# Attention with beacons and a soft mixture of experts: V loaded in fp16 through GpSimd's queue, its key order restored on TensorE, and TensorE's work in a new order

## The chip, the cores and the metric

The kernel runs on one core of one Trainium2 chip. The metric is device time in microseconds (us) of one execution. Before the change three runs gave 215.09, 217.38 and 217.65 us; the median is 217.38.

## The reference, cut to what matters

```
B, H, S, Nb, D = 8, 8, 576, 16, 64            # batches, heads, tokens, beacons, head width
k_all = concatenate([beacon_k, k], axis=2)    # 592 keys
v_all = concatenate([beacon_v, v], axis=2)
scores = q @ k_all.T / sqrt(D), causal over the 576, beacons always seen
a = softmax(scores);  attn = a @ v_all
x = attn as (B*S = 4608, H*D = 512)
logits = x @ phi                              # 32 slots, 4 for each of 8 experts
slot_input = softmax(logits over tokens).T @ x
slot_out = relu(slot_input[e] @ w1[e]) @ w2[e]   # w1 (512, 1024), w2 (1024, 512)
out = softmax(logits over slots) @ slot_out
```

All inputs and the output are float32.

## The kernel before

**Staging.** A batch has eight heads; they go in pairs, so there are 32 pairs, n = 0 to 31, and g = n % 4 is the pair's place in its batch. Keys are in five chunks of up to 128 (16 beacons and 576 tokens, the last chunk 80). `load_pair` (line 86) brings q and k of a pair on SyncE's queue; five pairs are in flight. `transp` (216) turns them on TensorE in bf16 into a PSUM buffer each, from which VectorE copies them to `qT` and `kT`, with the beacons' part from `bkT` (line 228). `bkT` is made once at the start by `beacons` (201), from `bkf`.

**Scores and attention.** `score(n, st)` (232) has four steps, which share two PSUM tiles `scs` in turn: step 2 needs what exp of step 0 has read, step 0 of the next pair what exp of step 2 has read. ScalarE takes exp of each step into `ex[n]`; GpSimd masks the diagonal blocks after steps 0 and 1. `attend(n, a)` (257) multiplies the 15 blocks of one head with `vh`, which holds V in fp16 and a column of ones per head; VectorE takes the reciprocal of the sums and scales into `xb`. Attention of pair n - 1 runs in iteration n.

**V.** `load_v` (100) loads V in float32 in the key order that attention needs, one chunk at a time: partition = key, so each packet is one row of 64 numbers, 256 bytes, on SyncE's queue. Beacon V comes apart. `cast_v` (277) turns each chunk to fp16 in `vh`: odd chunks on VectorE, even ones on GpSimd.

**Routing.** When a batch's eight heads are in `xb`, seven pieces follow (`routing`, 340): two transposes of two chunks (`xt_piece`) and one of the last, two halves of the logits with exp, the transposed weights (`dt_piece`) and the slot inputs (`si_piece`). They are queued in `work` and taken out between steps 0 and 1 of later iterations (lines 362 to 364): two in g = 1, three in g = 2, two in g = 3.

**PSUM.** Four banks hold the scores, two the attention, and two (`ps_tr`, tag `tr`, two buffers) are shared in turn by all transposes, logits and slot inputs.

**Weights.** `load_w` (129) loads the experts' weights with a cast to fp16 on GpSimd's queue, 24 full pieces during the loop after the schedule `want` (352), and 16 half pieces after the last iteration into buffers that q, k and V have left.

**The order** of every engine's work is the order of the program (`manual_schedule`, line 49); each engine takes its instructions in that order. The loop is in lines 357 to 404. After it come the experts (lines 408 to 460) and the output (464 to 478).

Of the kernel before, what the change touches and what calls it, by code (L numbers as in the profile page):

```python
# [17 lines left out]
def kernel(  # L18
# [12 lines left out]
    nc = tc.nc  # L31
# [37 lines left out]

    const = ctx.enter_context(tc.tile_pool(name="const", bufs=1))  # L70
    qkp = ctx.enter_context(tc.tile_pool(name="qkp", bufs=5))
    vfp = ctx.enter_context(tc.tile_pool(name="vfp", bufs=6))
    vbp = ctx.enter_context(tc.tile_pool(name="vbp", bufs=1))
    exq = ctx.enter_context(tc.tile_pool(name="exq", bufs=2))
    sml = ctx.enter_context(tc.tile_pool(name="sml", bufs=4))
    NW = 24
# [21 lines left out]
    vf = {}  # L98

    def load_v(b, cs):  # L100
        for c in cs:
            t = vfp.tile([P, H, D], FP, name="vf", tag="vf")
            vf[(b, c)] = t
            if c == 0 and b > 0:
                r0 = b * H * S - Nb
                nc.sync.dma_start(
                    out=t[:, :, :],
                    in_=v.rearrange("b h s d -> (b h s) d")[r0:r0 + H * S].rearrange(
                        "(h s) d -> s h d", s=S)[0:P])
            else:  # L110
                lo, hi = max(0, c * P - Nb), min(S, (c + 1) * P - Nb)
                p0 = lo + Nb - c * P
                nc.sync.dma_start(out=t[p0:p0 + hi - lo],
                                  in_=v[b, :, lo:hi, :].rearrange("h p d -> p h d"))
            if c == 0:
                vb = t
                if b > 0:
                    vb = vf[(b, "b")] = vbp.tile([P, H, D], FP, name="vb", tag="vb")
                nc.sync.dma_start(out=vb[0:Nb], in_=beacon_v[b].rearrange("h n d -> n h d"))

    NPC = 4 * E
    NH = 2 * (NPC - NW)
    wv = {}
    homes = ["qf", "kf", "vf", "vf"] * 2 + ["qf", "kf"] * 3 + ["vf", "vf"]
    assert len(homes) == NH

    def load_w(x):
        if x < NW:  # L130
            m, hs = x, (0, 1)
            t = wh.tile([P, 2048], F16, name="w", tag="w")
        else:
            m, hs = NW + (x - NW) // 2, ((x - NW) % 2,)
            tag = homes[x - NW]
            t = (vfp if tag == "vf" else qkp).tile(
                [P, 1024 if tag == "vf" else J * P], F16, name="wx", tag=tag)
# [18 lines left out]
    def w2c(e, t):  # L156
        o = (t % 2) * Dm
        return wv[(4 * e + 2 + t // 4, (t % 4) // 2)][:, o:o + Dm]

    load_pair(0)  # L160
    bkf = const.tile([P, B, D], FP, name="bkf")
    nc.sync.dma_start(out=bkf[:, :, :], in_=beacon_k.rearrange("b h n d -> (h n) b d"))
    load_pair(1)
    load_v(0, range(NCH))
# [4 lines left out]
    load_pair(4)  # L169


    idb = const.tile([P, P], BF, name="idb")
    make_identity(nc, idb)
# [103 lines left out]
    def cast_v(b, c):  # L277
        kn = P if c < 4 else UL
        (nc.vector if c % 2 else nc.gpsimd).tensor_copy(  # L279
            out=vh[b % 2][0:kn, c, :, 0:D], in_=vf.pop((b, c))[0:kn])  # L280
        if c == 0 and b > 0:
            nc.gpsimd.tensor_copy(out=vh[b % 2][0:Nb, 0, :, 0:D], in_=vf.pop((b, "b"))[0:Nb])
# [69 lines left out]
    def want(n):
        if n < 27:
            return int(0.66 * n)
        return {27: 19, 28: 21, 29: 23, 30: NW}.get(n, NW + NH)

    for n in range(NP + 1):
        b, g = divmod(n, H // 2)
        last = n == NP
        if not last:  # L360
            score(n, 0)
            for _ in range((0, 2, 3, 2)[n % 4]):
                if work:
                    work.pop(0)()
            score(n, 1)
# [9 lines left out]
        if not last:  # L375
            score(n, 2)
        if n >= 1:
            attend(n - 1, 1)
            if n % (H // 2) == 0:
                work += routing(n // (H // 2) - 1)  # L380
        if not last:
            score(n, 3)
        if last:
            while work:
                work.pop(0)()

        if not last:
            if g == 3 and b + 2 < B:
                load_v(b + 2, (0,))
            if b + 1 < B:  # L390
                load_v(b + 1, ((0, 1) if n == 0 else (1,), (2,), (3,), (4,))[g])
            if n + 5 < NP:
                load_pair(n + 5)
            if g == 0 and b > 0:
                cast_v(b, 3)
                cast_v(b, 4)
            if g == 2 and b + 1 < B:
                cast_v(b + 1, 0)
                cast_v(b + 1, 1)
            if g == 3 and b + 1 < B:  # L400
                cast_v(b + 1, 2)
            while wl < want(n):
                load_w(wl)
                wl += 1
    assert wl == NW + NH
# [103 lines left out]
```

## Time and profile before

| | |
|---|---|
| three runs | 215.09, 217.38, 217.65 us |
| the profiled execution | 215.74 us, of which the span on the engines is 214.0 |
| mean granted TensorE clock | 0.898 |
| DMA | 61,795 packets, 43,072 of them under 512 B; 55.86 MB |
| SyncE's queue (q, k, V, out) | 52,928 packets, 38.58 MB |
| GpSimd's queue (weights) | 8,832 packets, 16.78 MB |

Busy time by stage, us (each stage's length in brackets), with the granted clock of TensorE:

| stage | TensorE | VectorE | ScalarE | GpSimd | clock |
|---|---|---|---|---|---|
| 0 to 12 (12) | 4.15 | 5.80 | 2.44 | 2.86 | 1.00 |
| 12 to 20 (8) | 6.63 | 6.91 | 5.25 | 4.35 | 1.00 |
| 20 to 60 (40) | 34.75 | 29.12 | 30.36 | 20.38 | 0.96 |
| 60 to 100 (40) | 35.68 | 30.91 | 30.54 | 21.25 | 1.00 |
| 100 to 150 (50) | 43.90 | 38.48 | 36.08 | 28.50 | 0.97 |
| 160 to 185 (25) | 21.51 | 4.53 | 2.60 | 7.85 | 0.64 |
| 185 to 214 (29) | 12.51 | 13.41 | 11.72 | 0.00 | 0.68 |

How to read the lines of a profile: a group of instructions is given with its source line, its engine, the operation, what it writes and reads (partitions x elements), how often it occurs, the total and the mean time, and the idle time of the engine just before it with what ended that wait. In order of time a line begins with start and length in us. A matmul's end is modelled and neighbouring ones overlap, so the spacing of starts tells more of TensorE than the sum of lengths.

### The profile page before, as it was taken

Reading aid. Unit: us, or ns where it says so; the run is one execution under the profiler, and the core shown is the slowest. Engines: PE = TensorE matmul, PEld = TensorE weight load, DVE = VectorE, ACT = ScalarE, POOL = GpSimd, SP = SyncE. Lnnn points to the kernel's source line nnn. Section 1 sums busy time; section 2 is a strip of 40 time slices with the busy share of each in tenths; the row PEclk is TensorE's granted clock in tenths of the full one; section 3 lists DMA queues with packets and bytes.
Section 4 is the critical chain, followed back from the end, with each engine's and each line's share of the span. In section 5 each row is a group of like instructions: output and inputs, shape, how many; then the busy total and the mean of one; then the engine's idle time right before and its main releaser. Section 6 shows DMA issues by size and latency. Waiting matters only on the chain.

```text
span 214.0 us, 8069 instructions
## 1 busy us (share of the span) xinstructions
PE 168.1 (79%) x3512; PEld 118.0 (55%) x3512; DVE 135.5 (63%) x339; ACT 127.5 (60%) x187; POOL 90.0 (42%) x144
## 2 busy tenths in 40 slices
PE   0579985989989888998798799899986799898200
PEld 0447664666667666766566676676764745333000
DVE  4576996378678967877797786769655300189400
ACT  2076983679778777876767787766871011189300
POOL 5052924554465463375535644658545430000000
PEclk9999999699999999999999999969999655569855
DMA  6999999999999999999999999999999999169996
GB/s 188 246 280 256 302 264 270 279 272 240 296 311 237 261 292 300 249 291 243 261 293 280 290 257 278 308 202 196 194 211 182 209 209 206 24 281 404 406 408 266
DMA packets 61795, 55.86 MB, mean 261 GB/s; under 512 B 43072, under 2 KB 43072, under 8 KB 61760
## 3 DMA queue, kind: packets, MB, share of 16 engines
q1 hardware_dynamic: 52928, 38.58, 61.3%
q0 software_dynamic: 8832, 16.78, 43.0%
q8 instruction: 27, 0.44, 0.8%
q14 instruction: 8, 0.07, 0.1%
HBM read 62.69 MB, written 9.44 MB: 337 GB/s over the span
## 4 chain that ended last, share of the span: by engine, by line
PE 43%; DVE 26%; ACT 11%; DMA 6%; issue 5%; POOL 1%; DVEq 0%; SPq 0%; ACTq 0%
ACT ex L244 11%; PE sc L238 10%; PE tr L223 7%; PE av L265 6%; DVE xb L273 5%; DVE qT L225 4%; DVE xT L300 4%; DVE kT L225 4%; PE tr L310 4%; PE av L433 4%; DMA vf<-in_v_dram 4%; PE tr L425 4%; PE tr L295 3%; PE fp L471 2%; PE tr L333 2%
## 5 line engine op out<-in xcount | busy, mean ns | idle before, releaser
L244 ACT ACTIVATE ex<-sc 128x1024 f16<-128x1024 f32 (+3 forms) x128 | 106.8, 869 | 45.1 <-PE sc L238 44.7
L246 POOL TENSOR_SCALAR_AFFINE_SELECT ex<-ex 128x1024 f16<-128x1024 f16 x32 | 34.9, 1090 | 51.0 <-ACT ex L244 51.0
L238 PE MATMUL sc<-qT,kT 64*128 64x128 bf16 (+5 forms) x576 | 47.8, 260 | 10.7 <-ACT ex L244 5.1
L265 PE MATMUL av<-vh,ex 128*128 128x65 f16 (+2 forms) x960 | 45.4, 200 | 3.0 <-POOL vh L279 1.9
L265 PEld LDWEIGHTS <-ex 128*128 128x128 f16 (+2 forms) x960 | 37.5, 108 | 9.9 <-issue 8.1
L225 DVE COPY qT<-tr 128x576 bf16<-128x576 bf16 x32 | 24.2, 756 | 21.9 <-PE tr L223 21.7
L238 PEld LDWEIGHTS <-kT 64*128 64x128 bf16 (+1 forms) x576 | 20.9, 103 | 24.9 <-issue 16.1
L273 DVE TENSOR_TENSOR xb<-av,r 128x320 f16<-128x320 f32 x64 | 31.5, 492 | 2.2
L225 DVE COPY kT<-tr 128x576 bf16<-128x576 bf16 x32 | 23.9, 748 | 0.1
L279 POOL CAST vh<-vf 128x512 f16<-128x512 f32 (+1 forms) x24 | 14.6, 611 | 15.4 <-DMA vf<-in_v_dram 15.4
L146 POOL DMA_DIRECT2D w<-in_moe_w_dram x24 | 17.3, 720 | 0.0
L223 PE MATMUL tr<-idb,kf 64*64 64x64 bf16 x576 | 15.6, 198 | 1.4 <-DVE bkT L210 0.4
L223 PEld LDWEIGHTS <-qf 64*64 64x64 bf16 x576 | 12.6, 112 | 6.1 <-issue 4.5
L223 PE MATMUL tr<-idb,qf 64*64 64x64 bf16 x576 | 15.8, 199 | 0.1
L272 DVE RECIPROCAL r<-av 128x5 f32<-128x5 f32 x64 | 12.1, 189 | 5.8 <-PE av L265 5.6
L223 PEld LDWEIGHTS <-kf 64*64 64x64 bf16 x576 | 13.6, 113 | 2.5 <-issue 2.2
L473 ACT ACTIVATE osb<-fp,rc 128x512 f32<-128x512 f32 x18 | 11.7, 685 | 5.1 <-PE fp L471 4.4
L252 POOL TENSOR_SCALAR_AFFINE_SELECT ex<-ex 80x160 f16<-80x160 f16 x32 | 10.3, 323 | 10.1 <-ACT ex L244 7.9
L471 PE MATMUL fp<-soh,eLh 128*128 128x512 f16 x36 | 12.2, 452 | 2.2 <-ACT osb L473 1.3
L476 DVE TENSOR_SCALAR osb<-fp,rc 128x512 f32<-128x512 f32 x18 | 12.7, 747 | 1.8 <-PE fp L471 1.4
L295 PE MATMUL tr<-idh,xb 128*128 128x128 f16 (+1 forms) x160 | 12.3, 218 | 1.1 <-DVE xb L273 0.8
L146 POOL DMA_DIRECT2D wx<-in_moe_w_dram x16 | 8.5, 544 | 8.0 <-DMA wx<-in_moe_w_dram 5.2
(57 smaller groups left out, 139.5 us busy)
## 6 DMA issues: line engine op xcount, KB each, us to landing
w<-in_moe_w_dram POOLq DMA_DIRECT2D x24, 512.0 KB, 8.5
qf<-in_q_dram SPq DMA_DIRECT2D x32, 288.0 KB, 7.4
kf<-in_k_dram SPq DMA_DIRECT2D x32, 288.0 KB, 6.9
out_dram<-osb SPq DMA_DIRECT2D x18, 512.0 KB, 5.4
vf<-in_v_dram SPq DMA_DIRECT2D x31, 256.0 KB, 6.9
wx<-in_moe_w_dram POOLq DMA_DIRECT2D x16, 256.0 KB, 9.7
vf<-in_v_dram SPq DMA_DIRECT2D x8, 160.0 KB, 7.2
bkf<-in_beacon_k_dram SPq DMA_DIRECT2D x1, 256.0 KB, 3.9
```

The source lines that it names most:

```text
L146: nc.gpsimd.dma_start(out=t[:, 0:1024 * len(hs)].rearrange("p (c f) -> p c f", f=1024), in_=src)
L223: nc.tensor.transpose(tp[po:po + 64, j, :], hi, idb[po:po + 64, po:po + 64])
L225: nc.vector.tensor_copy(out=dst[:, Nb:Nb + S].rearrange("p (s j) -> p s j", j=J), in_=tp[:, :, :].rearrange("p j s -> p s j"))
L238: nc.tensor.matmul(sc[0:kn, a, col:col + un], kT[n % 3][64 * a:64 * a + 64, P * c:P * c + kn], qT[n % 3][64 * a:64 * a + 64, u0:u0 + un], ...
L244: nc.scalar.activation(ex[n][:, :, o:o + w], sc[:, :, 0:w], AF.Exp, scale=scale)
L246: nc.gpsimd.affine_select(out=ex[n][:, :, 0:512].rearrange("p a (c t) -> p a c t", c=4), in_=ex[n][:, :, 0:512].rearrange("p a (c t) -> p ...
L265: nc.tensor.matmul(avs[a][0:m, i * DD:(i + 1) * DD], ex[n][0:kn, a, o:o + m], vh[b % 2][0:kn, c, h, :], start=(c == 0), stop=(c == i))
L273: nc.vector.tensor_tensor(out=xb[b % 2][:, :, h, :], in0=avv[:, :, 0:D], in1=r5[:, :].unsqueeze(2).broadcast_to([P, NCH, D]), op=AL.mult)
L279: (nc.vector if c % 2 else nc.gpsimd).tensor_copy(out=vh[b % 2][0:kn, c, :, 0:D], in_=vf.pop((b, c))[0:kn])
L295: nc.tensor.transpose(tp[:, ii, t, 0:m], xb[b % 2][0:m, i, 2 * t:2 * t + 2, :].rearrange("p h d -> p (h d)"), idh[0:m, 0:m])
L471: nc.tensor.matmul(fp_[:, :], etok(cg, j), soh[:, :], start=True, stop=True)
L476: nc.vector.tensor_scalar(out=osb[:, j - j0, :], in0=fp_[:, :], scalar1=rc[:, i:i + 1], scalar2=None, op0=AL.mult)
```

## The change

V is loaded by `load_v` as a tile `vq` of 128 partitions with four neighbouring keys each, cast to fp16 on the way, by two DMAs per batch on GpSimd's queue; each packet reads 1 KB. It covers the first four chunks; the last 80 keys (`vl`) still come in float32 on SyncE's queue and GpSimd casts them. For batches after the first the tile starts 16 rows early, so that partition p holds keys 4p to 4p + 3 of the concatenated order; for the first batch it starts at partition 4 (124 partitions). Since key 4p + s lies in partition p, chunk c is in partitions 32c to 32c + 31, and `sel_piece` brings it in order: for each s a product with a 0/1 matrix `sel` (32 rows, 128 columns) over all 512 numbers of the eight heads, four products added up in PSUM, for two chunks at a time in alternation, and VectorE copies the sums to `vh`. Beacon V comes by eight DMAs on GpSimd's queue at the start and is copied into its 16 places by VectorE. `sel` is made at the start by a memset, four fills on GpSimd and a last memset of its first four rows on VectorE.

The loop is written anew. Step 0 of the next pair is issued at the end of an iteration, before the loads; attention stands behind steps 2 and 3 rather than ahead of them; the seven pieces of routing have places of their own (`slot`): ahead of step 1 ("pre"), ahead of step 3 ("mid") and at the end ("end"). `sel_piece` stands at the end of g = 2 and g = 3, for the next batch; for the first batch both stand in iteration 0 ahead of step 2. Two more weight pieces (26 in all) go into full-size buffers, 12 half pieces remain.

```diff
-    vfp = ctx.enter_context(tc.tile_pool(name="vfp", bufs=6))
-    vbp = ctx.enter_context(tc.tile_pool(name="vbp", bufs=1))
+    vqp = ctx.enter_context(tc.tile_pool(name="vqp", bufs=2))
+    vlp = ctx.enter_context(tc.tile_pool(name="vlp", bufs=2))
...
+    def load_v(b):
+        t = vqp.tile([P, H, 4, D], F16, name="vq", tag="vq")
+        vq[b] = t
+        p0 = Nb // 4 if b == 0 else 0
+        if b == 0:
+            nc.vector.memset(t[0:32], 0.0)
+        r0 = b * H * S - (Nb if b > 0 else 0)
+        rows = v.rearrange("b h s d -> (b h s) d")[r0:r0 + H * S].rearrange(
+            "(h p j) d -> p h j d", h=H, j=4)[0:P - p0]
+        for h0 in range(0, H, H // 2):
+            nc.gpsimd.dma_start(out=t[p0:P, h0:h0 + H // 2], in_=rows[:, h0:h0 + H // 2])
...
+    idb = const.tile([P, P], BF, name="idb")
+    make_identity(nc, idb)
     load_pair(0)
+    bvh = const.tile([P, 2, H, D], F16, name="bvh")
+    for b in range(B):
+        o = 32 * (b % 4)
+        nc.gpsimd.dma_start(out=bvh[o:o + Nb, b // 4], in_=beacon_v[b].rearrange("h n d -> n h d"))
+    load_v(0)
...
+    sel = const.tile([P, 4, P], F16, name="sel")
+    nc.vector.memset(sel[:, :, :], 0.0)
+    for c in range(4):
+        nc.gpsimd.affine_select(
+            out=sel[32 * c:32 * c + 32, :, :], in_=sel[32 * c:32 * c + 32, :, :],
+            compare_op=AL.not_equal, fill=1.0, base=0, pattern=[[-1, 4], [1, P]],
+            channel_multiplier=-4)
+    nc.vector.memset(sel[0:Nb // 4, :, :], 0.0)
...
+    def sel_piece(b, cs):
+        t = vq[b]
+        tps = [ps_tr.tile([P, H, D], FP, name="tr", tag="tr") for c in cs]
+        for s in range(4):
+            for c, tp in zip(cs, tps):
+                nc.tensor.matmul(tp[:, :, :], sel[32 * c:32 * c + 32, s, :],
+                                 t[32 * c:32 * c + 32, :, s, :],
+                                 start=(s == 0), stop=(s == 3))
+        for c, tp in zip(cs, tps):
+            nc.vector.tensor_copy(out=vh[b % 2][:, c, :, 0:D], in_=tp[:, :, :])
+        if 0 in cs:
+            o = 32 * (b % 4)
+            nc.vector.tensor_copy(out=vh[b % 2][0:Nb, 0, :, 0:D], in_=bvh[o:o + Nb, b // 4])
...
+    def place(b):
+        n0 = (b + 1) * (H // 2)
+        for i, (dn, w) in enumerate(((1, "mid"), (1, "end"), (2, "pre"), (2, "mid"), (3, "mid"),
+                                     (4, "pre"), (4, "mid"))):
+            places[(n0 + dn, w)] = routing(b)[i]
...
+    score(0, 0)
+    for n in range(NP):
         b, g = divmod(n, H // 2)
...
+        slot(n, "pre")
+        score(n, 1)
         if n + 1 < NP:
             transp(n + 1)
         if n == 0:
-            for c in range(NCH):
-                cast_v(0, c)
+            cast_vl(0)
+            sel_piece(0, (0, 1))
+            sel_piece(0, (2, 3))
...
+        score(n, 2)
         if n >= 1:
             attend(n - 1, 0)
-        if not last:
-            score(n, 2)
+        slot(n, "mid")
+        score(n, 3)
         if n >= 1:
             attend(n - 1, 1)
...
+            if g == 0:
+                place(b - 1)
+        slot(n, "end")
+        if g >= 2 and b + 1 < B:
+            sel_piece(b + 1, ((0, 1), (2, 3))[g - 2])
+        if n + 1 < NP:
+            score(n + 1, 0)
+
+        if n == 0:
+            load_v(1)
+        if g == 2 and b + 2 < B:
+            load_v(b + 2)
+        if g == 0 and b + 1 < B:
+            load_vl(b + 1)
...
```

More of the change, by code (lines that the diff above doesn't have):

```diff
@@ L94, in load_pair @@
             d[n] = t
[L98 to L119, printed above, removed]
+    vq, vl = {}, {}
@@ L123, with load_vl @@
+    def load_vl(b):
+        t = vlp.tile([P, H, D], FP, name="vl", tag="vl")
+        vl[b] = t
+        nc.sync.dma_start(out=t[0:UL], in_=v[b, :, S - UL:S, :].rearrange("h p d -> p h d"))
     NPC = 4 * E
-    NH = 2 * (NPC - NW)
+    NV = NW + 2
     wv = {}
-    homes = ["qf", "kf", "vf", "vf"] * 2 + ["qf", "kf"] * 3 + ["vf", "vf"]
-    assert len(homes) == NH
+    homes = ["qf", "kf"] * 5 + ["vl", "vl"]
+    NH = len(homes)
+    assert NH == 2 * (NPC - NV)
     def load_w(x):
-        if x < NW:
+        if x < NV:
@@ L131, in load_w @@
             m, hs = x, (0, 1)
-            t = wh.tile([P, 2048], F16, name="w", tag="w")
+            t = (wh if x < NW else vqp).tile([P, 2048], F16, name="w", tag="w" if x < NW else "vq")
         else:
[L134 to L137, printed above, removed]
+            m, hs = NV + (x - NV) // 2, ((x - NV) % 2,)
+            tag = homes[x - NV]
@@ L138, in load_w @@
+            t = (vlp if tag == "vl" else qkp).tile(
+                [P, 1024 if tag == "vl" else J * P], F16, name="wx", tag=tag)
         e, r = divmod(m, 4)
@@ L163 @@
     load_pair(1)
-    load_v(0, range(NCH))
+    load_vl(0)
     phif = const.tile([P, NDC, NSL], FP, name="phif")
@@ L169 @@
     load_pair(4)
-    idb = const.tile([P, P], BF, name="idb")
-    make_identity(nc, idb)
     idh = const.tile([P, P], F16, name="idh")
     nc.vector.tensor_copy(out=idh[:, :], in_=idb[:, :])
+    sel = const.tile([P, 4, P], F16, name="sel")
[6 more added lines that the diff above has]
+    nc.vector.memset(sel[0:Nb // 4, :, :], 0.0)
     ones = const.tile([P, 1], F16, name="ones")
@@ L275, in attend, with cast_vl @@
             in1=r5[:, :].unsqueeze(2).broadcast_to([P, NCH, D]), op=AL.mult)
[L277 to L282, printed above, removed]
+    def cast_vl(b):
+        nc.gpsimd.tensor_copy(out=vh[b % 2][0:UL, 4, :, 0:D], in_=vl.pop(b)[0:UL])
+    def sel_piece(b, cs):
[11 more added lines that the diff above has]
+            nc.vector.tensor_copy(out=vh[b % 2][0:Nb, 0, :, 0:D], in_=bvh[o:o + Nb, b // 4])
     xT = {}
@@ L344, in routing, with slot @@
                 lambda: dt_piece(b), lambda: si_piece(b)]
+    places = {}
+    def place(b):
[3 more added lines that the diff above has]
+            places[(n0 + dn, w)] = routing(b)[i]
+    def slot(n, w):
+        f = places.pop((n, w), None)
+        if f is not None:
+            f()
     beacons()
     transp(0)
-    work = []
     wl = 0
@@ L354, in want @@
             return int(0.66 * n)
-        return {27: 19, 28: 21, 29: 23, 30: NW}.get(n, NW + NH)
-    for n in range(NP + 1):
+        return {27: 19, 28: 21, 29: 23, 30: 25}.get(n, NV + NH)
+    score(0, 0)
+    for n in range(NP):
         b, g = divmod(n, H // 2)
-        last = n == NP
-        if not last:
[L361 to L365, printed above, removed]
+        slot(n, "pre")
+        score(n, 1)
         if n + 1 < NP:
@@ L368 @@
         if n == 0:
-            for c in range(NCH):
-                cast_v(0, c)
+            cast_vl(0)
+            sel_piece(0, (0, 1))
+            sel_piece(0, (2, 3))
             for r in range(4):
                 nc.vector.tensor_copy(out=phih[:, :, r, :], in_=phif[:, :, :])
+        score(n, 2)
         if n >= 1:
             attend(n - 1, 0)
-        if not last:
-            score(n, 2)
+        slot(n, "mid")
+        score(n, 3)
         if n >= 1:
             attend(n - 1, 1)
[L379 to L405, printed above, removed]
+            if g == 0:
[11 more added lines that the diff above has]
+            load_vl(b + 1)
+        if n + 5 < NP:
+            load_pair(n + 5)
+        if g == 3 and b + 1 < B:
+            cast_vl(b + 1)
+        while wl < want(n):
+            load_w(wl)
+            wl += 1
+    attend(NP - 1, 0)
+    slot(NP, "pre")
+    attend(NP - 1, 1)
+    slot(NP, "mid")
+    assert not places
+    for f in routing(B - 1):
+        f()
+    assert wl == NV + NH
     dsum = const.tile([P, 1], FP, name="dsum")
```

## The prediction

> **What bounds the kernel now.** I read the page's shares first, then the waits, then the instructions in order of time in the middle of the run and at its start.
>
> ```profile
> PE 168.1 (79%) x3512; PEld 118.0 (55%) x3512; DVE 135.5 (63%) x339; ACT 127.5 (60%) x187; POOL 90.0 (42%) x144
> DMA  6999999999999999999999999999999999169996
> ```
>
> No engine is full over the span, and the DMA engines are nearly always busy. Whether anybody waits for them is read from the waits (total us, times, longest):
>
> ```profile
> ACT ex L244 <- PE sc L238: 44.7, 69, 8.8
> POOL vh L279 <- DMA vf<-in_v_dram: 15.4, 6, 5.2
> PE av L265 <- POOL vh L279: 1.9, 1, 1.9
> ```
>
> GpSimd's wait for V reaches TensorE once, for 1.9 us. The 44.7 us in which ScalarE waits for scores are the loss. One iteration of the head-pair loop shows how they arise:
>
> ```profile
> 69.83 0.40 PE L238 MATMUL sc<-qT,kT 64*128 64x128 bf16 x8 [0.23 <-ACT ex L244]
> 70.17 1.19 PE L295 MATMUL tr<-idh,xb 128*128 128x128 f16 x16
> 70.35 1.02 ACT L244 ACTIVATE ex<-sc 128x1024 f16<-128x1024 f32 x1 [0.16 <-PE sc L238]
> 70.95 1.29 DVE L300 COPY xT<-tr 128x1024 f16<-128x1024 f16 x2 [0.21 <-PE tr L295]
> 71.28 0.41 PE L238 MATMUL sc<-qT,kT 64*80 64x80 bf16 x6
> 71.73 1.00 ACT L244 ACTIVATE ex<-sc 128x992 f16<-128x992 f32 x1 [0.36 <-PE sc L238]
> 72.29 0.47 PE L223 MATMUL tr<-idb,kf 64*64 64x64 bf16 x18
> 72.69 0.67 PE L265 MATMUL av<-vh,ex 128*128 128x65 f16 x15
> 73.30 0.37 PE L238 MATMUL sc<-qT,kT 64*128 64x464 bf16 x2
> 73.71 1.35 ACT L244 ACTIVATE ex<-sc 128x928 f16<-128x928 f32 x2 [0.97 <-PE sc L238]
> ```
>
> Routing (line 295) stands between step 0 and step 1 of the scores; its copies hold both `tr` buffers, so the transposes of k (72.29) wait; step 2 comes late and ScalarE idles 0.97. The step-0 products start at 66.39, 69.83, 74.70, 80.04 and (exp of step 2 ends there) about 84.75: the iteration without routing takes 3.44 us, those with it 4.87, 5.34 and 4.7, together 18.4 per group of four. So the loop is bound by TensorE's order and its hand-overs, not by DMA.
>
> **The change part by part.** V's DMA: 256-byte packets (most of the 43,072 under 512 B) become a quarter as many of 1 KB. By the waits above nobody but GpSimd stood behind them, save at 34 to 36 us, where ScalarE lost 3.05. I count this edit at nothing; its cover is the issue five iterations ahead of q and k and 7.4 us to land. If the cover failed it would be worth that 3 us. The casts of V leave VectorE (two of 478 ns per batch) and GpSimd (three of about 610 and one of 606; one stays).
>
> **The start.** Here the change adds a wait.
>
> ```profile
> 1.44 2.02 POOL L192 MEMSET hTz<- 128x2048 f16 x1
> 5.68 0.76 DVE L204 CAST bkd<-bkf 128x512 bf16<-128x512 f32 x2 [1.78 <-DMA bkf<-in_beacon_k_dram]
> 10.19 1.02 PE L238 MATMUL sc<-qT,kT 64*128 64x128 bf16 x14 [0.93 <-DVE kT L228]
> 12.25 0.91 PE L238 MATMUL sc<-qT,kT 64*128 64x464 bf16 x4
> 14.51 1.02 PE L238 MATMUL sc<-qT,kT 64*128 64x128 bf16 x14 [1.35 <-DVE kT L228]
> ```
>
> GpSimd now issues eight DMAs of beacon V and two of V before it fills `sel`. Its rows: 544 ns for a DMA of 128 packets, 720 for one of 256, so 1.4 ns per packet more. Eight of 128 packets: 4.3 us; two of 496: 544 + 368 x 1.4 = 1.06 each, 2.1. One fill of `sel` (512 elements, between 323 ns for 160 and 1,090 for 1,024): 0.64. From 1.4 us on, that ends at 8.4. VectorE's clearing of `sel[0:4]` waits for it, and behind it in VectorE's queue stand the memsets (some 0.75 us) and the casts of `bkf`: 9.2 instead of 5.68. From there to the first scores is a chain (casts, transposes, copies), so they shift by **+3.5** (0 if the wait is passed over, +5.4 if all four fills are waited for).
>
> In iteration 0 TensorE must now do both `sel_piece` calls before step 2, in its order. No row shows a 32-row product with 512 columns. Nearest are line 433's products (512 columns, four side by side): eight take 1.04 us, one 0.62, so a round takes 0.42 at the granted clock of 0.50 there, and 0.21 at full clock. The 464-column pair on 64 rows each (two in 0.37, one in 0.385) shows row halves side by side too. A piece is four rounds: 0.85, or 1.7 on the slow array of the start (a block of 15 attention products takes 1.06 at 18 us and 0.67 later); twice that if the two rows of tiles don't run together. I take side by side. Each piece leaves two copies of 128x512 f32 out of PSUM, 0.75 each (line 476: 747). Unshifted, the transposes' buffers are free at 13.3; piece one runs to 15.0, its copies from 15.3 to 16.05 and 16.8; piece two needs those buffers and runs to 18.5. Step 2 stands there instead of at 12.25; from it to the next step 0 were 2.3 us (line 228's copy), now 1.6 (0.6 to exp, 0.94 exp): **+5.5**; at full clock +3.5.
>
> V(0) must have landed by 16.8 in the shifted time. It is issued by 7.9 and DMAs of GpSimd took 8.5 median: just hidden. The row: every V transfer before covers 112, 128 or 80 partitions and landed in 4.6 to 11.9 us. The Trainium skill ("DMA: Bandwidth & Descriptors", section on why a DMA increments its semaphore by 16) says that the engines used are the largest number up to 16 that divides the slowest dimension, though GpSimd's copies sometimes get 16 anyway. By that, V(0), with 124 partitions, might use four; no run here shows it. By the rows the sum holds nothing for it; by the page's strict reading it would be 234, the case of a late V below.
>
> The early stall (3.05 us of ScalarE): V(1) is asked for at the end of iteration 0 and needed in iteration 2, some 8 us later, so some of it comes back: **-1** (-3 to +3).
>
> **The loop.** TensorE's spacing by the timeline: step 0 0.33, step 1 0.34, transposes 0.69, step 2 0.30, attention 0.60 twice, step 3 0.22: 3.1 per iteration. Routing per four: 0.6 and 0.6 and 0.2 (line 295), 1.05 (line 310), 0.6 (322 and 333): 3.0. `sel` 1.7. In the new order a plain iteration still ends with step 0 waiting for exp of step 2: 3.5. Walking through the four: g0 has dt, which waits 0.7 for the first copy of the `sel` piece before it, and the q transposes wait for the second; 4.7. g1 has 16 transposes in the open: 4.4. g2 has the last transposes, a logit and a piece: 4.9. g3 has q and k transposes waiting for two copies (+0.8), a logit and a piece: 5.2. Together 19.2, against 18.4: **+0.8 per group**. Without `sel` the same walk gives about 16.5, so the order is worth -1.9 and `sel` costs +2.7 (1.7 of products, 1.0 of buffer waits). VectorE's 2.1 us more per group (four copies of 0.75 and a small one, less two of 0.48) lie beside, save where those waits are. Six groups with `sel`: +4.8; the last has none: -1.9; the first has the products but no routing: +1.5. Sum **+4.4**. Bounds: all PE work back to back, 12.4 + 3.0 + 1.7 = 17.1 (-1.3 per group), and +1.5 per group with the pauses of 0.3 to 0.5 that TensorE's issue shows now.
>
> **The end.** From 168 to 185 us TensorE does 1.92 us per expert at clock 0.5, and out is written at 406 GB/s: nothing changes. Eight weight pieces' worth less one come after the loop, behind that cover: 0.
>
> Sum: 3.5 + 5.5 - 1 + 4.4 = +12.4 on the profiled execution's 215.74 (span 214.0 and 1.74 around it): **228**. That execution lies 1.6 below the median of 217.38, inside the three runs.
>
> **The rivals.** *The order wins (faster).* TensorE's waits take up the pieces, groups come to 17.1 (-1.3 x 7 = -9), the start costs its low ends (+3.5) and the stall goes (-3): 207. For it: 44.7 us of ScalarE's idle time to gain. Against: two `tr` buffers serve everything. It decides below 17.7 us per group. Chance 0.15.
>
> *The two cancel.* Groups stay at 18.4, the start costs +3.5 and the stall stays: 219. Chance 0.15.
>
> *V(0) lands late.* Its 124 partitions don't divide evenly over 16 engines; if its 1.02 MB go over four of them, at 25 GB/s each (406 over 16), they need 10 us alone and 20 shared with q and k, so it lands at 18 to 28 rather than by 16.8, middle +6: 234. Against: no V transfer was that slow. This is the case of the skill's rule above. Chance 0.12.
>
> *The pieces don't run side by side.* Then 0.85 more per piece, 14 pieces, and 3.4 at the start: +15, 243. Chance 0.05.
>
> **How the numbers follow.** The forecast has 0.53, with its own range 221 to 236 from the loop's and the start's bounds. A measurement here tells about 2%, 213.0 to 221.7. Faster 0.15, same 0.15, slower 0.70. The range takes in the forecast, the cancelling case and the late V, 214 to 240, and leaves out 0.2.
>
> **What would show it.** The first scores near 13.7 us, with VectorE waiting for GpSimd's `sel`; step 2 of iteration 0 near 22; groups of four step-0 starts near 19.2; q and k transposes right after a piece waiting for VectorE; ScalarE's wait for scores still the largest. The forecast is wrong if the first scores stay at 10, or if groups fall under 17.7.

## The result and the profile after

| | median us | range | against the kernel before |
|---|---|---|---|
| before | 217.04 | 215.09 to 217.65 | |
| after | 236.79 | 234.40 to 238.33 | 1.0949, 95% interval 1.0846 to 1.1052 |

The change makes the kernel slower, by 9.5%. The profiled execution after is the one of 238.33, with a span of 236.6. Ratios here and below are taken over undisturbed executions alone, so they need not be the quotient of two medians; of the profiled executions, the one after and those of order_only, order_v_early, early and no_sel below lie 3.9 to 5.3 us above the shortest of their kernel.

The page's busy line and its DMA row after:

```profile
PE 181.7 (77%) x3640; PEld 122.7 (52%) x3640; DVE 149.4 (63%) x366; ACT 126.3 (53%) x187; POOL 97.7 (41%) x147
DMA  7999019596999999999999999975799999929997
```

TensorE has 13.6 us more to do (the products with `sel` alone 19.7 by their lengths), VectorE 13.9, and the DMA engines, full all through before, are nearly idle in two slices of the start (24 to 36 us) and have some room from about 148 to 166. Whatever the new V loading saved there, the time did not follow. The waits (us in all, times, longest):

```profile
ACT ex L256 <- PE sc L250: 64.0, 42, 14.4
...
PE tr L299 <- DMA vq<-in_v_dram: 8.5, 2, 7.3
DVE sel L187 <- POOL sel L183: 8.2, 1, 8.2
...
PE tr L345 <- DVE vh L303: 2.7, 6, 0.5
```

ScalarE's wait for scores grows from 44.7 to 64.0 us, but it comes in fewer pieces, and one of them is 14.4 us long. GpSimd no longer waits 15.4 us for V; TensorE now waits for V itself, once for 7.3 us. Where the time goes in the course of the run is read from marks that every kernel here has: the starts of GpSimd's mask of step 0 (line 246 before, 258 after) for pairs 0, 1, 5 and 31, the casting of `siT` that follows the loop, and the writing of `soh` that ends the experts.

| us | pair 0 | pair 1 | pair 5 | pair 31 | `siT` | `soh` | span |
|---|---|---|---|---|---|---|---|
| before | 11.93 | 16.25 | 36.42 | 157.28 | 167.57 | 185.36 | 214.0 |
| after | 17.55 | 33.62 | 55.67 | 176.84 | 187.29 | 208.12 | 236.6 |
| later by | 5.6 | 17.4 | 19.2 | 19.6 | 19.7 | 22.8 | 22.6 |

So 17.4 of 22.6 us are lost before pair 1, 1.9 more up to pair 5, 0.3 in the 26 iterations that follow, and 3.0 between `siT` and `soh`. The start, in order of time (start, length, instruction, idle time before it and its releaser):

```profile
6.69 3.08 POOL L111 DMA_DIRECT2D vq<-in_v_dram  x2 [0.83 <-DMA bvh<-in_beacon_v_dram]
...
10.53 0.27 DVE L187 MEMSET sel<- 4x256 uint32 x1 [8.22 <-POOL sel L183]
...
15.80 1.02 PE L250 MATMUL sc<-qT,kT 64*128 64x128 bf16 x14 [0.93 <-DVE kT L240]
...
25.24 1.89 PE L299 MATMUL tr<-vq,sel 32*128 32x512 f16 x8 [7.32 <-DMA vq<-in_v_dram]
...
27.89 2.46 PE L299 MATMUL tr<-vq,sel 32*128 32x512 f16 x8 [0.75 <-DVE vh L303]
...
30.27 0.74 PE L250 MATMUL sc<-qT,kT 64*128 64x464 bf16 x4
...
34.67 1.56 POOL L111 DMA_DIRECT2D vq<-in_v_dram  x2
...
41.50 1.04 PE L299 MATMUL tr<-vq,sel 32*128 32x512 f16 x8 [1.20 <-DMA vq<-in_v_dram]
```

VectorE waits 8.22 us for GpSimd's first fill of `sel`, and the first scores come at 15.80 instead of 10.19. Then TensorE stands 7.32 us until V(0), the V of batch 0, is there (16.6 us from issue to landing; the other `vq` loads take 6.1). Two pieces follow, and step 2 of iteration 0 runs at 30.27 instead of 12.25. V(1) is asked for only at 34.67: its two DMAs stand in GpSimd's queue behind the mask of pair 1 (33.62), and the first piece of batch 1 waits for them at 41.50.

The stretch after that, in windows of 6 us (length; busy time and instructions of TensorE, its weight loads, VectorE, ScalarE and GpSimd; granted clock, DMA share, GB/s):

```profile
42.00:48.00 6.00, 5.66 (x94) 3.67 (x92) 4.65 (x10) 3.37 (x4) 3.60 (x5) 0.68 0.56 128
48.00:54.00 6.00, 6.00 (x94) 4.05 (x92) 3.85 (x9) 3.37 (x4) 1.92 (x3) 0.50 1.23 234
```

TensorE is busy here at half its clock for part of the first window and all of the second. A normal iteration with a piece, at 99 us:

```profile
99.03 1.04 PE L299 MATMUL tr<-vq,sel 32*128 32x512 f16 x8
...
100.00 0.61 PE L250 MATMUL sc<-qT,kT 64*128 64x128 bf16 x14
100.10 1.29 DVE L303 CAST vh<-tr 128x512 f16<-128x512 f32 x2 [0.24 <-PE tr L299]
100.52 2.75 ACT L256 ACTIVATE ex<-sc 128x1024 f16<-128x1024 f32 x3 [1.24 <-PE sc L250]
...
100.85 0.47 PE L235 MATMUL tr<-idb,qf 64*64 64x64 bf16 x18 [0.24 <-DVE vh L303]
```

A piece takes TensorE 0.97 us (99.03 to 100.00), the transposes of q wait 0.24 for the first copy, those of k (101.45) for the second, and ScalarE is idle for 1.24 because the piece stands ahead of step 0. The periods of a quiet group are 4.20, 4.88, 5.01 and 4.34 us, together 18.43; the group of the kernel before that the prediction walks through took 18.4. In the mean, the six groups from pair 5 to pair 29 take 18.84 after and took 18.53 before. And the end, where the experts wait for the last half pieces of the weights:

```profile
202.50 0.94 PE L462 MATMUL tr<-siT,wx 128*128 128x4 f16 x29 [0.95 <-DMA wx<-in_moe_w_dram]
...
206.22 0.61 PE L470 MATMUL av<-wx,hTz 128*32 128x512 f16 x2 [0.64 <-DMA wx<-in_moe_w_dram]
207.47 0.61 PE L470 MATMUL av<-wx,hTz 128*32 128x512 f16 x2 [0.64 <-DMA wx<-in_moe_w_dram]
```

### The profile page after: what moved, and what is told of

The parts are those of the page before. It is cut to its first block, busy times and chain, and to the rows that moved or that the text cites. A ratio compares the mean times of both kernels' runs of the same rounds, so it can differ in the third digit from the quotient of the medians.

```text
span 236.6 us, 8309 instructions
## 1 busy us (share of the span) xinstructions
PE 181.7 (77%) x3640; PEld 122.7 (52%) x3640; DVE 149.4 (63%) x366; ACT 126.3 (53%) x187; POOL 97.7 (41%) x147
## 2 busy tenths in 40 slices
DMA packets 40003, 51.57 MB, mean 218 GB/s; under 512 B 13120, under 2 KB 21280, under 8 KB 39968
## 4 chain that ended last, share of the span: by engine, by line
PE 47%; DMA 22%; DVE 10%; issue 6%; ACT 5%; POOL 4%; ACTq 0%; POOLq 0%; DVEq 0%
PE av L277 14%; DMA wx<-in_moe_w_dram 10%; PE sc L250 10%; DMA vq<-in_v_dram 10%; PE tr L299 8%; PE tr L235 6%; ACT ex L256 5%; DVE vh L303 4%; PE fp L508 3%; PE tr L333 2%; PE tr L318 2%; DMA bvh<-in_beacon_v_dram 2%; DVE osb L513 2%; DVE xT L323 1%; PE tr L356 1%
## 5 line engine op out<-in xcount | busy, mean ns | idle before, releaser
L256 ACT ACTIVATE ex<-sc 128x1024 f16<-128x1024 f32 (+3 forms) x128 | 105.7, 870 | 64.9 <-PE sc L250 64.0
L250 PE MATMUL sc<-qT,kT 64*128 64x128 bf16 (+5 forms) x576 | 45.1, 260 | 4.8 <-ACT ex L256 3.8
L277 PEld LDWEIGHTS <-ex 128*128 128x128 f16 (+2 forms) x960 | 38.3, 109 | 11.8 <-issue 8.6
L303 DVE CAST vh<-tr 128x512 f16<-128x512 f32 x32 | 20.7, 689 | 15.0 <-PE tr L299 15.0
L299 PE MATMUL tr<-vq,sel 32*128 32x512 f16 x128 | 19.7, 422 | 9.3 <-DMA vq<-in_v_dram 8.5
L284 DVE RECIPROCAL r<-av 128x5 f32<-128x5 f32 x64 | 12.9, 202 | 9.7 <-PE av L277 8.7
L144 POOL DMA_DIRECT2D w<-in_moe_w_dram x26 | 18.6, 717 | 0.0
L235 PEld LDWEIGHTS <-qf 64*64 64x64 bf16 x576 | 14.0, 113 | 7.6 <-issue 7.1
L235 PEld LDWEIGHTS <-kf 64*64 64x64 bf16 x576 | 13.7, 114 | 2.2 <-issue 2.2
L508 PE MATMUL fp<-soh,eLh 128*128 128x512 f16 x36 | 12.6, 467 | 2.0 <-ACT osb L510 1.2
L111 POOL DMA_DIRECT2D vq<-in_v_dram x16 | 13.7, 855 | 0.8 <-DMA bvh<-in_beacon_v_dram 0.8
L513 DVE TENSOR_SCALAR osb<-fp,rc 128x512 f32<-128x512 f32 x18 | 12.8, 749 | 1.8 <-PE fp L508 1.3
L299 PEld LDWEIGHTS <-sel 32*128 32x128 f16 x128 | 5.5, 98 | 16.1 <-issue 12.4
## 6 DMA issues: line engine op xcount, KB each, us to landing
vq<-in_v_dram POOLq DMA_DIRECT2D x2, 248.0 KB, 16.6
```

The lines of the kernel that those rows point to most:

```text
L144: nc.gpsimd.dma_start(out=t[:, 0:1024 * len(hs)].rearrange("p (c f) -> p c f", f=1024), in_=src)
L235: nc.tensor.transpose(tp[po:po + 64, j, :], hi, idb[po:po + 64, po:po + 64])
L250: nc.tensor.matmul(sc[0:kn, a, col:col + un], kT[n % 3][64 * a:64 * a + 64, P * c:P * c + kn], qT[n % 3][64 * a:64 * a + 64, u0:u0 + un], ...
L256: nc.scalar.activation(ex[n][:, :, o:o + w], sc[:, :, 0:w], AF.Exp, scale=scale)
L277: nc.tensor.matmul(avs[a][0:m, i * DD:(i + 1) * DD], ex[n][0:kn, a, o:o + m], vh[b % 2][0:kn, c, h, :], start=(c == 0), stop=(c == i))
L299: nc.tensor.matmul(tp[:, :, :], sel[32 * c:32 * c + 32, s, :], t[32 * c:32 * c + 32, :, s, :], start=(s == 0), stop=(s == 3))
```

## The experiments

The theory after this reading: the start loses by V(0)'s slow landing, the wait for `sel` and the pieces; in the loop the order's gain and the pieces' price cancel; V(1) and the last weights are asked for too late. The rivals: one of the halves of the change alone makes the loss, or the loop would have gained if DMA had kept up. The marks of all profiled executions, to be read with each experiment:

| us | pair 0 | pair 1 | pair 5 | pair 31 | `siT` | `soh` | span | pairs 5 to 31 |
|---|---|---|---|---|---|---|---|---|
| before | 11.93 | 16.25 | 36.42 | 157.28 | 167.57 | 185.36 | 214.0 | 120.9 |
| after | 17.55 | 33.62 | 55.67 | 176.84 | 187.29 | 208.12 | 236.6 | 121.2 |
| order_only | 12.04 | 16.37 | 32.72 | 159.61 | 169.89 | 190.29 | 218.9 | 126.9 |
| v_only | 17.64 | 34.21 | 51.14 | 185.12 | 195.40 | 212.30 | 240.8 | 134.0 |
| v0_split | 17.92 | 27.32 | 48.75 | 168.95 | 179.43 | 200.27 | 228.8 | 120.2 |
| v0_halves | 20.66 | 32.68 | 50.81 | 172.42 | 182.87 | 203.82 | 232.3 | 121.6 |
| sel_pool | 16.02 | 33.59 | 53.07 | 174.10 | 184.60 | 205.22 | 233.7 | 121.0 |
| no_sel | 17.95 | 35.09 | 55.94 | 167.10 | 177.55 | 198.85 | 227.4 | 111.2 |
| sel_act | 17.41 | 33.07 | 51.54 | 173.06 | 183.50 | 204.23 | 232.7 | 121.5 |
| early | 15.75 | 23.69 | 40.71 | 164.11 | 174.62 | 195.06 | 223.6 | 123.4 |
| early_w | 15.65 | 24.07 | 41.34 | 165.93 | 176.20 | 193.05 | 221.6 | 124.6 |
| early_w_act | 15.51 | 22.78 | 39.07 | 164.34 | 174.61 | 191.52 | 220.1 | 125.3 |
| v0_old | 12.93 | 17.45 | 44.76 | 169.82 | 180.09 | 196.95 | 225.6 | 125.1 |
| order_v_early | 11.89 | 16.21 | 32.30 | 160.72 | 170.99 | 189.94 | 218.7 | 128.4 |

**V(0) in two parts (v0_split).** The 124 partitions of V(0) are loaded as 112 and 12.

```diff
+        cuts = (p0, P) if b > 0 else (p0, p0 + 112, P)
         for h0 in range(0, H, H // 2):
-            nc.gpsimd.dma_start(out=t[p0:P, h0:h0 + H // 2], in_=rows[:, h0:h0 + H // 2])
+            for lo, hi in zip(cuts, cuts[1:]):
+                nc.gpsimd.dma_start(out=t[lo:hi, h0:h0 + H // 2],
+                                    in_=rows[lo - p0:hi - p0, h0:h0 + H // 2])
```

> V(0)'s 124 partitions are loaded as 112 and 12, four DMAs instead of two; nothing else changes. Theory (124 partitions go over few of the DMA engines): V(0) lands within 9 us of its issue, the first sel product stands near 18 instead of 25.2 us, and the time falls by 6 to 7, to about 230. Rival (V(0) is late because q and k use the engines): the first product stays within 1.5 us of 25.2 and the time within 2 us of 236.8.

Measured: 232.94 (230.5 to 235.63), ratio to before 1.0645 (1.0516 to 1.0775). V(0) lands after 9.3 us instead of 16.6, and the first piece and step 2 come 6.6 and 6.3 us sooner:

```profile
18.68 2.52 PE L302 MATMUL tr<-vq,sel 32*128 32x512 f16 x8 [0.37 <-DVE qT L240]
...
23.98 0.74 PE L253 MATMUL sc<-qT,kT 64*128 64x464 bf16 x4
```

The time falls by 3.9 in the median and 7.8 between the profiled executions; the next wait for V(1) is longer (3.0 us). So up to pair 1 the slow landing is worth what was expected (33.62 to 27.32, 6.3 us), and the longer wait for V(1) takes part of it back. The packets of GpSimd's queue from 8 to 24 us (packets, MB, share of 16 engines' time), after and then v0_split:

```profile
q0 software_dynamic: 4371, 0.56, 46.6%
```

```profile
q0 software_dynamic: 1594, 0.57, 29.0%
```

The same bytes go in 2.7 times as many packets. Over the whole run the kernel after has 2,912 packets more under 512 bytes (13,120 against 10,208), as many from 512 bytes to 2 KB (8,160 in both), and no more than 0.01 MB more: the rows of V are whole, and small packets come on top. The trace records the size of each packet: all that come on top have 4 bytes.

**The count of partitions (v0_halves).** The same with 62 and 62.

```diff
-        cuts = (p0, P) if b > 0 else (p0, p0 + 112, P)
+        cuts = (p0, P) if b > 0 else (p0, p0 + 62, P)
```

> V(0) as two loads of 62 partitions in place of 112 and 12. With 124 partitions it landed after 16.6 us and the kernel sent 13,120 packets below 512 bytes, with 112 and 12 after 9.3 us and 10,208. If a count of partitions that is no multiple of 16 is what breaks the rows up, there are some 13,100 small packets again and V(0) lands after 14 to 17 us. If it is the size of the load, about 10,200, 9 to 11 us, and a time near that of v0_split (230 to 236).

Measured: one execution of 234.04; V(0) lands after 13.7 us, and the first piece waits 3.26 us for it. The same window:

```profile
q0 software_dynamic: 8377, 0.58, 66.3%
```

Under 512 bytes there are 17,120 packets, more than with 124 and more than either case foresaw, and again 8,160 above. So it isn't the size of the load: with two loads of 112 it goes in few packets, with 124 or 62 partitions in many. GpSimd's queue has 16 packets of 4 bytes for any load (640 for the 40 loads of the kernel before). What comes on top of these is 2,976 for the two loads of 124 partitions, 6,944 for the four of 62, and 32 for the two of 112 and the two of 12 together. So it is the count of partitions, neither the size nor the number of the loads; what the small packets are for is not shown.

**The wait for `sel` (sel_pool).** The last clearing of `sel` on GpSimd instead of VectorE.

```diff
-    nc.vector.memset(sel[0:Nb // 4, :, :], 0.0)
+    nc.gpsimd.memset(sel[0:Nb // 4, :, :], 0.0)
```

> The last clearing of sel's first rows goes from VectorE to GpSimd, so VectorE waits for nothing of sel. Theory (V(0)'s landing sets the start, the wait on sel is hidden behind it): the first scores move from 15.8 to about 11 us, but the first sel product stays at 25 and the time within 1.5 us of 236.8. Rival (both add up, as the prediction had it): 4 to 5 us less, about 232.

Measured: 236.48 (235.45 to 238.27), ratio 1.09 (1.0802 to 1.0998): nothing against the kernel after.

```profile
10.61 1.02 PE L250 MATMUL sc<-qT,kT 64*128 64x128 bf16 x14 [1.04 <-DVE kT L240]
...
25.21 1.89 PE L299 MATMUL tr<-vq,sel 32*128 32x512 f16 x8 [12.48 <-DMA vq<-in_v_dram]
```

The first scores are back at 10.61, and TensorE waits 12.48 us for V(0) instead of 7.32. The wait for `sel` is real and hidden behind V(0).

**The order alone (order_only).** V loaded and cast as before, TensorE's work in the new order; the five chunks are cast where the two pieces stood in iteration 0, and later chunks are asked for and cast in the iterations in which the kernel before does it.

> The loads and casts of V as before the change, with TensorE's new order alone; no sel products. Theory (the walk of the prediction): groups of four take 16.5 us instead of 18.4, some 13 us less in the loop than before: about 204. Rival (with the order improved the 256-byte packets of V bind the loop): groups stay near 18, 214 to 217, with GpSimd's or TensorE's wait for V grown well above 15.4 and 1.9 us.

Measured: 220.61 (12 runs, 215.26 to 226.12) against 217.37, ratio 0.997 (0.9927 to 1.0014): the same. Iterations take 3.79 us where V is there, but single ones take 5.1 to 12.8 (in the profiled execution, of 220.59; the five shortest took 215.3 to 215.8):

```profile
PE av L265 <- POOL vh L279: 11.9, 6, 3.5
...
POOL vh L279 <- DMA vf<-in_v_dram: 10.9, 5, 6.1
```

GpSimd waits for V and TensorE for GpSimd. The rival held in the main: a faster order asks for V sooner than it comes, and TensorE's wait grew from 1.9 to 11.9 us, though GpSimd's fell from 15.4 to 10.9. Behind the longest of these waits TensorE ran at a granted clock of 0.50 (72 to 78 and 132 to 138 us), so not all that was lost is waiting.

**V asked for sooner, with the old loading (order_v_early).**

```diff
-            load_v(b + 1, ((0, 1) if n == 0 else (1,), (2,), (3,), (4,))[g])
+            load_v(b + 1, ((0, 1, 2) if n == 0 else (1, 2), (3,), (4,), ())[g])
```

> The old V loads and casts in the new order (order_only, 220.6 us against 217.4 before), with each V chunk asked for one iteration sooner: chunks 1 and 2 at a group's start, 3 in its second iteration, 4 in its third. In order_only the iterations took 3.79 us when V was there, and single iterations of 5.1 to 12.8 us stood between them. Theory 1: V comes late because its last chunks are asked for late; then the long iterations vanish, groups go to 16 us, and the time to 203 to 210. Theory 2: the DMA engines cannot move the small packets of V any faster; then the waits move to an earlier chunk, groups stay near 18 us, and the time stays within 4 us of 217.

Measured: 218.15 (216.48 to 220.37), beside 218.47 for the kernel before on that chip. Its page's DMA row, and four of its waits:

```profile
DMA  6999999999999999999999999999999999369996
```

```profile
PE av L265 <- POOL vh L279: 9.2, 6, 5.4
...
POOL vh L279 <- DMA vf<-in_v_dram: 5.9, 2, 4.6
...
PEld L223 <- DMA qf<-in_q_dram: 2.9, 3, 1.2
...
PEld L223 <- DMA kf<-in_k_dram: 2.7, 4, 1.6
```

The waits for V shrink by a quarter and by half, the iterations from pair 5 to pair 31 do not (128.4 us against 126.9). Instead TensorE's weight loads wait for q and k, 2.9 and 2.7 us where it was 0.7 and 0.6 in order_only. Theory 2 held, with this difference that the waits moved to q and k and not to an earlier chunk of V: what one load gains by being asked for earlier, others lose. So the kernel before stood closer to the limit of its DMA than its waits showed. The DMA row alone does not show it, for it is as full in the loop of the kernel after.

**The loading alone (v_only).** V by GpSimd's queue and `sel`, the pieces at the same places, all else in the old order.

> V in fp16 with sel products, in TensorE's old order (sel products at the end of the third and fourth iteration of a group, after step 3). Theory (sel costs 2.7 us per group whatever the order): groups near 21, seven of them, about 15 to 18 us more than with both changes: 252 to 255. Rival (the order is worth little): within 4 us of 236.8.

Measured: 244.25 (242.52 to 247.98), ratio 1.1222 (1.1113 to 1.1332). It lies between the two expectations. From pair 5 to 31 it takes 134.0 us against 121.2 after: with the new loading the order is worth 12.8 us over 6.5 groups, 2.0 each. Up to pair 5 it is 4.5 ahead of the kernel after, where the old order asks for V(1) at 19.53 and not at 34.67, and neither a wait for V(1) nor a clock below 1.00 follows up to 60 us.

**The pieces left out (no_sel).** From batch 2 on the products with `sel` and their copies are left out, and those batches use the V of batches 0 and 1 for their first 512 keys.

```diff
-        if g >= 2 and b + 1 < B:
+        if g >= 2 and b + 1 < 2:
```

> The changed kernel without sel products and copies from batch 2 on (12 pieces; those batches use the V of batches 0 and 1 for their first 512 keys). Theory (sel costs 2.7 us per group, 1.7 of products and 1.0 of waits): 16 us less, about 221, plain groups near 16. Rival (only the products' own time): 10 us less, about 227, groups near 16.8.

Measured: 227.64 (two runs, 225.02 and 230.26), 9.2 below after, so the rival's time came. The quiet stretches are those of the theory: four iterations without a disturbance take 15.6 to 16.1 us against 18.43, so a group's two pieces cost 2.3 to 2.9 there, and by the same numbers the order without pieces is worth 2.3 to 2.8 per group (18.4 less 15.6 to 16.1). Over the whole stretch from pair 5 to pair 31 both are smaller: 111.2 us against 121.2 after and 120.9 before, 1.5 per group each. Part is given back, in iterations of 5.1 to 5.6 us that come with pauses of TensorE for which the profile shows no releaser (1.09 us before 71.70, 1.55 before 123.31) and with a lower granted clock; and its experts take 21.3 us (`siT` to `soh`). order_only has the same order with the old loading and takes 126.9 from pair 5 to pair 31: in the new order the new loading does gain time, and the pieces take most of it back.

**One of the copies on ScalarE (sel_act).**

```diff
-        for c, tp in zip(cs, tps):
-            nc.vector.tensor_copy(out=vh[b % 2][:, c, :, 0:D], in_=tp[:, :, :])
+        nc.vector.tensor_copy(out=vh[b % 2][:, cs[0], :, 0:D], in_=tps[0][:, :, :])
+        nc.scalar.activation(vh[b % 2][:, cs[1], :, 0:D], tps[1][:, :, :], AF.Copy)
```

> The changed kernel with the second of a sel piece's two copies on ScalarE instead of VectorE. Theory (a third of sel's price in the loop is the wait of the q and k transposes, or of dt, for VectorE's two copies in a row): the iterations after a piece get 0.3 to 0.5 us shorter, 4 to 7 us in all: 230 to 233. Rival (the price is the products' own time, and ScalarE's copy delays exp of step 0): within 2 us of 236.8 or slower.

Measured: 234.77 (232.68 to 235.87), ratio 1.0812 (1.0691 to 1.0933), 2.0 below after. The iterations that follow a piece become 4.86 and 4.19 instead of 5.01 and 4.34. The rival was nearer: the second copy holds the transposes of k only by 0.15 us an iteration, and the stretch from pair 5 to pair 31 is no shorter for it (121.5 against 121.2), because single other iterations are longer. The ratio's interval overlaps that of the kernel after, so the 2.0 us are not clear of noise. That the rest of the piece's price is TensorE's own time and the late step 0 is argued, not shown.

**The start put right (early), and the weights sooner (early_w).** V(0) as 112 and 12 partitions, V(0) and `sel` ahead of beacon V in GpSimd's queue, `sel` cleared on GpSimd, V(1) asked for ahead of step 0 of pair 1. early_w has also:

```diff
-            return int(0.66 * n)
-        return {27: 19, 28: 21, 29: 23, 30: 25}.get(n, NV + NH)
+            return int(0.9 * n)
+        return {27: 26, 28: 28, 29: 30, 30: 32}.get(n, NV + NH)
```

> The changed kernel with four moves at the start: V(0) in 112 and 12 partitions, its DMAs and then the making of sel ahead of beacon V's DMAs on GpSimd, sel cleared on GpSimd, V(1) asked for ahead of step 0 of pair 1. Theory (the start is a chain of V(0)'s landing, the late V(1) and the slow clock that its stall leaves): first scores near 10.6, the first sel product near 14 to 16, the step-0 mask of pair 1 near 22 instead of 33.6, no stall at V(1): 14 to 16 us less than the change, 221 to 223. Rival (the rest of the start is DMA-bound): the first product not before 18 and 228 or more.

> As early, and the weights asked for sooner (0.9 per iteration, then two half pieces per iteration from the 28th on). Theory (the experts wait 3 us for the last pieces, because they are asked for late while the DMA engines idle): 2.5 to 4 us less than early, and no wait for weights in the experts' stage. Rival (the weights' arrival is bound by the DMA engines): as early within 1 us.

Measured: early 224.01 (221.36 to 225.27), ratio 1.0286 (1.017 to 1.0402), 12.8 below after; early_w 222.17 (221.28 to 223.27), ratio 1.0244 (1.0159 to 1.0329). early falls a little short of its theory (14 to 16 us less), and early_w lies between its theory and its rival, 1.8 below early with overlapping intervals. In early_w no matmul waits for weights, and `siT` to `soh` takes 16.9 us against 20.8 after and 20.4 in early. The start of early_w:

```profile
12.92 1.02 PE L253 MATMUL sc<-qT,kT 64*128 64x128 bf16 x14 [0.94 <-DVE kT L243]
...
15.42 2.52 PE L302 MATMUL tr<-vq,sel 32*128 32x512 f16 x8 [0.38 <-DVE qT L240]
17.53 1.53 POOL L113 DMA_DIRECT2D vq<-in_v_dram  x2
...
20.72 0.74 PE L253 MATMUL sc<-qT,kT 64*128 64x464 bf16 x4
```

No product waits for V any more, and step 2 comes 9.6 us sooner than after; the pieces themselves (15.42 to 20.72) remain. The first scores come at 12.92 and not near 10.6, since VectorE now waits 5.5 us for `bkf` (1.8 before). Part of the gain goes in the loop, 124.6 us against 121.2 after and 123.4 in early. In early_w the loads of k land after 8.3 us instead of 5.7 (6.2 in early), with the weights beside them, and TensorE's weight loads wait for k (after, then early_w):

```profile
PEld L235 <- DMA kf<-in_k_dram: 0.3, 2, 0.2
```

```profile
PEld L238 <- DMA kf<-in_k_dram: 1.7, 5, 1.0
```

This wait covers a part of the 3.4 us; the rest is not explained.

**Both together (early_w_act).** early_w with the copy on ScalarE.

> Both of the earlier gains in one kernel: early_w (222.2 us) with the second copy of each piece on ScalarE (sel_act, 2.0 us below the changed kernel). If the two add, 220.2, groups some 0.3 us shorter; if ScalarE's step 0 is late behind that copy once TensorE waits less, 222 or above.

Measured: 221.58 (220.53 to 222.58), 0.6 below early_w; from pair 5 to 31 it takes 125.3 us. The two gains hardly add, and the 0.6 lies within the spread of the runs.

**Batch 0 the old way (v0_old).** early_w_act with V(0) loaded and cast as in the kernel before, so that the products start with batch 1.

> early_w_act (221.6 us) with batch 0's V loaded and cast as in the kernel before, so that batch 0 needs neither sel nor its products; sel is filled on GpSimd before the first step 0, V(1) is asked for behind the casts of V(0), and the products start with batch 1. If the rest of the loss is the start alone, pair 1's first step 0 comes at 16.3 to 17.5 us as before (24.1 in early_w) and groups stay at some 18.1, so 214 to 217: level with the kernel before or up to 3 us below. If V(0)'s small packets (5 chunks in single precision) hold up q, k and V(1), the start gains 3 or less and V(1) stalls TensorE at the second iteration's end: 219 to 222.

Measured: 229.55 (226.2 to 231.28), ratio 1.056 (1.0428 to 1.0691). Pair 1 comes at 17.45 as expected, and then:

```profile
15.93 1.53 POOL L113 DMA_DIRECT2D vq<-in_v_dram  x2
...
30.75 1.89 PE L297 MATMUL tr<-vq,sel 32*128 32x512 f16 x8 [6.83 <-DMA vq<-in_v_dram]
```

```profile
20.00:24.00 4.00, 3.79 (x91) 2.94 (x89) 3.38 (x11) 2.93 (x4) 3.34 (x7) 1.00 1.18 315
24.00:28.00 4.00, 0.00 (x0) 0.00 (x0) 0.64 (x2) 0.23 (x1) 0.00 (x0) 1.00 1.18 311
28.00:32.00 4.00, 1.25 (x7) 0.51 (x8) 0.00 (x0) 0.00 (x0) 0.00 (x0) 0.50 0.84 98
```

V(1) takes 12.6 us to land, on full DMA engines (share above 1 until 28 us) among the loads of q, k, the last keys of V and beacon V, and TensorE stands for 6.8 us, with all others behind it. The rival named the mechanism; its price was higher than 219 to 222. The start's loss was not removed but moved by one batch. No version tried is shown to be faster than the kernel before.

## Why the prediction was right, and where its terms were not

Direction and range held (slower; 236.8 in 214 to 240), but 228 was 8.8 short of the median, and the forecast's own range of 221 to 236 was missed by 0.8. That the miss was not larger is in part luck: the loop was put 4.1 us too high, which made up for some of what the start and the end were put too low. The terms against the profiled executions:

| term | predicted | measured |
|---|---|---|
| start, `sel` ahead of the casts | +3.5 | +5.6, but covered by V(0) |
| V(0) | hidden | 7.3 beyond that |
| two pieces in iteration 0 | +5.5 | the rest of 17.4, 4.5 |
| early stall, V(1) | -1 | +1.9 |
| loop | +4.4 | +0.3 |
| end | 0 | +3.0 |

**The step that failed is V(0), "just hidden".** It was costed by the landing of other loads, though no row showed one with 124 partitions; it took 16.6 us. That case stood among the rivals with a chance of 0.12 and a time of 234, and it is what happened; v0_split and v0_halves show that the count of partitions made it. Whether it came by the mechanism written there, few engines, stays open, but the counts of packets speak for it.

The Trainium skill ("DMA: Bandwidth & Descriptors", section on why a DMA increments its semaphore by 16) gives four engines for 124 partitions, with the exception that GpSimd's copies may get 16. An estimate by that rule: 62 partitions would go over two engines, 12 over twelve and 112 over all 16; and if each engine without rows got one packet of 4 bytes for every row that one with rows carries, there would be 12 x 124 = 1,488 for a load of 124 partitions (496 rows, 124 on each of four), 14 x 124 = 1,736 for one of 62 (248 rows), 4 x 4 = 16 for one of 12 (48 rows) and none for one of 112. For the loads of the three kernels that makes 2,976, 6,944 and 32, which is what the traces have. The exception, with eight partitions on each of 15 engines and four on the last, would give 16 for a load of 124.

Which engine carried a packet the trace does not say, so the four engines are not shown. The time of the packets does not decide it: from 14 to 20 us those of GpSimd's queue took 80.8% of the time of all 16 engines for 0.35 MB, but 33.6 points of it are the 4-byte packets, and the DMA share comes to 1.37 in a window (12 to 18 us), so one engine's time can be counted more than once. Nor is it shown whether few engines or the packets on top make the load slow. What the runs show is that a load of 124 partitions goes in 2.7 times as many packets and lands 7.3 us later than one of 112 and 12.

**The `sel` wait** was right in kind (VectorE waits 8.22 us for GpSimd) and too small: GpSimd stood 0.83 us before the issue of V(0) for an earlier DMA, and that issue took 3.08 us rather than 2.1; the first fill took 0.65, as assumed. sel_pool shows that it cost nothing with V(0) so late.

**The pieces of iteration 0** were right: side by side, 25.24 to 30.27, 5.0 us, where the working had 5.2 from piece one to step 2. The rival of pieces one after the other fell: eight products take 1.04 us in the loop. At 25.24 they take 1.89, as the working had it for the slow array of the start. TensorE had stood for 7.32 us before, but that is not shown to be the reason: single products take 626 ns in the median there, and as long in v0_split, whose first piece waited 0.37 us. The Trainium skill ("TensorE: Matmul & The Clock Gate", part 1) has the array at half speed by default and again after some 3.4 us of idleness; no run here tells the two apart. The granted clock in the rows reads 1.00 there, and the lengths decide.

**V(1)** went the other way. The step that the prediction left out is a queue: `load_v(1)` now stands behind the mask of pair 1 on GpSimd, and that mask waits for everything in iteration 0. The stall itself is 1.2 us on TensorE; the half clock from 42 to 54 us follows it. sel_act has the same stall (1.43) without a clock below 1.00 behind it, and goes from pair 1 to pair 5 in 18.5 us against 22.05: so the half clock makes 3 to 4 us of this execution, the slowest of the four after. early asks for V(1) ahead of the mask, has no stall, and takes 17.0.

**The loop** was predicted at 19.2 per group with the order at -1.9 and the pieces at +2.7. Measured in quiet groups are 18.43, -2.3 to -2.8 and +2.3 to +2.9 (no_sel), which cancel: the rival "the two cancel" was right for the loop. v_only gives 2.0 for the order, and the whole stretch of no_sel 1.5 for each. The mechanism (products and waits for two `tr` buffers) held, and the price of the pieces is about right; the term that was mis-sized is the group. Iteration by iteration the walk gave 4.7, 4.4, 4.9 and 5.2 for g = 0 to 3, and 4.34, 4.20, 4.88 and 5.01 were measured: most is missing in g = 0, where `dt` waits 0.45 us in the mean for the copy (2.7 in six) and not 0.7.

**The end** was called covered. The weights that fall behind the loop are not: between 156 and 168 us the DMA engines were only at 0.59, while the schedule of `want` held the requests back. early_w asks sooner and takes 3.5 us off the experts' stretch of early (20.4 to 16.9), though only 1.8 off its time.

One part of the reading of the kernel before was too simple: "bound by TensorE's order and its hand-overs, not by DMA". By order_only and order_v_early the transfers were, with the old loading, a second bound right behind the first. The change removes it as far as no_sel goes (four iterations in 15.6 to 16.1 us with the new loading), and pays for it on TensorE, which is the first.

## What to carry to other kernels

A cheaper transfer gains nothing while another engine sets the pace, and work on that engine that restores the order of the data has to be earned back by something else: here order and products weigh some 2 us per group each. For a new load shape look for the landing time of exactly that shape, and for what stands ahead of its issue in its queue; both moved the time more than the whole loop did. Where one bound is taken away, look which one stands right behind it: full DMA engines without a wait can be such a one, and asking for one load earlier and watching the waits of the others tells whether they are.

## What the runs showed of the hardware

- A casting load on GpSimd's queue with 124 partitions landed after 16.6 us and with 62 + 62 after 13.7, with 112 + 12 after 9.3; the bytes were equal (0.56 to 0.58 MB in the window), the packets 4,371, 8,377 and 1,594. All that came on top are packets of 4 bytes: 1,488 for each load of 124 partitions, 1,736 for each of 62. The two issues of 124 partitions took 3.08 us, one of 112 took 0.72, two of 128 some 1.5.
- A short stall was followed, or not, by a stretch at half clock. The stalls for V(1) of 2.99 (v0_split), 2.42 (no_sel) and 6.83 us (v0_old) were; those of 1.20 to 1.43 us were followed by windows of 6 us at 0.68 and 0.50 (after), by one at 0.72 (sel_pool), and by none below 1.00 (sel_act). The five kernels with the new loading that do not wait for V(1) had 1.00 from 36 to 54 us. What decides it was not tested. At the start the row does not show the slow array: in the kernel after it reads 1.00 up to 42 us, while 18 transposes take 0.69 us at 32.85 and 0.47 at 37.53.
- A copy of 128x512 float32 out of TensorE's sums took VectorE 0.69 us and ScalarE 0.60.
